# Strassen for a third unit, and the spectral steps moved one unit earlier

## The chip, the cores and the metric

One core of a Trainium2 chip runs the kernel. The metric is the device time of one execution in microseconds (us), lower is better. TensorE is called PE in the profile, its weight loads PEld, VectorE DVE, ScalarE ACT, GpSimd POOL and SyncE SP.

## The reference

The input `x` is (8, 3008, 256): batch, tokens, channels. All is float32.

```python
X = np.fft.rfft(x, axis=1)                         # over the 3008 tokens
Yr = Xr @ w_r - Xi @ w_i + b_r                     # mix of the 256 channels
Yi = Xr @ w_i + Xi @ w_r + b_i
Yr, Yi = soft_threshold(Yr, 0.01), soft_threshold(Yi, 0.01)
y = np.fft.irfft(Yr + 1j * Yi, n=3008, axis=1)     # (8, 3008, 256)
h = np.maximum(y.transpose(0, 2, 1) @ w_tok1, 0) @ w_tok2   # 3008 -> 256 -> 3008 tokens
u = y + h.transpose(0, 2, 1)
out = u + np.maximum(u @ w_ch1, 0) @ w_ch2         # 256 -> 1536 -> 256 channels
```

## The kernel before, in words

The eight batches form five units: unit 0 is batch 0, unit 1 is batch 1, units 2, 3 and 4 are pairs of batches. To hold float32 accuracy on the fast matmul format, an operand is split into a high and a low part, and a product is three matmuls (`mm3`, lines 191 to 194, so the profile names most matmuls by these lines and by their tiles).

Each unit passes two phases.

The *spectral phase* (`spectral`, with the closures of `parts`). First comes the transform `dft47`, a Fourier transform of length 47 in 13 groups. A group loads `x` (480 KB for a pair of batches, SP's queue, three buffers of tag `ld`), forms sums and differences (`sum_diff`, GpSimd and VectorE), splits them (`split_x`, ScalarE and VectorE), runs six matmuls (`stage1`, tile `p`), copies them out with ScalarE (tile `a`, line 265, two buffers of tag `ev`) and stores `a` to DRAM (`a_d`, line 267, ScalarE's queue). Unit 1 is half as wide. Then come 12 pairs of frequencies `kp`, for each batch: `forward` (tile `px`, line 465, then `xf`, `xth`, `xtl` by ScalarE, GpSimd, ScalarE and VectorE), `mix` (tiles `pm`), and once for each `kp` `inverse` (tiles `pi`, stored to `b_d`) and `tokens` (tile `gp`). `mix` of a step follows the `forward` of the next one. `close` turns `gp` into the hidden tokens `gh` and `gl`.

The *channel phase* (`channel`). `make_u` builds `u` from `gh`, `gl`, the second token weights `wt2` and `b2`, loaded from `b_d` (tile `pu`). A chunk of up to 512 tokens then takes, for each of 12 blocks of 128 hidden channels, six matmuls for the first layer (tile `ph`), a rectification and split (`hh` line 810, `hlo` line 811) and six matmuls for the second (tile `po`). The units of `SEVEN`, the last ones, use `channel7` instead: chunks of 1024 tokens, and the first layer as Strassen's scheme in Winograd's form, with seven products in place of eight (tiles `sx`, `sw`, `sq`, `sz`). It needs sums of the weights (`weigh`) and of `u` (`sum_u`, `split_u7`) and sums of the products (`first7`), done on VectorE and ScalarE. These units' tiles live in the pool `seven`, which `open_seven` opens where the spectral tiles were, so all spectral work must be over by then.

The order in each engine's queue is written out by the program. Unit 0's spectral phase stands alone at the start (`begin`), beside weight preparation. After that the spectral steps of later units are dealt out between pieces of the channel phase. `BESIDE` says whose steps run beside which unit. A loop at the end keeps `left_s` (spectral work left, by the plan 70.3 us a batch) and `left_c` (channel work left until the unit's last chunk), and after each channel piece emits steps:

```python
            while left_s > pace * left_c:
                step = next(sp, None)
                if step is None:
                    left_s = -1e9
                elif step == "wait":
                    hold = left_c - 10.0
                    break
                else:
                    left_s -= step
```

`pace` is `left_s / left_c`, taken anew after each hold. A step tells its planned time: 1.4 for a group of a pair unit's transform (0.7 for unit 1), 0.9 for `forward`, 2.15 for `mix`, 0.68 a batch for `inverse`, 1.37 a batch for `tokens`. A "wait" holds the spectral steps until 10 us of planned channel work have been emitted; before the change there is one, after each transform, for the way of `a` through DRAM. A chunk of 512 counts 32.7, a `make_u` 3.6 for 470 tokens. At "end", what is left of the steps is emitted at once. The first hold, in unit 0, is 25.

The hidden tokens of one unit at a time lie in the two tiles `gh` and `gl` of the pool `const`; those of units 3 and 4 are stored to DRAM (`g_d`) when made, and loaded by `fetch_g` when their channel phase comes.

Of the kernel before, what the change touches and what calls it, by code (L numbers as in the profile page):

```python
# [11 lines left out]
F32 = mybir.dt.float32  # L12
# [5 lines left out]
B, N, C = 8, 3008, 256  # L18
# [5 lines left out]
UNITS = [[0], [1]] + [[2 * p, 2 * p + 1] for p in range(1, NP)]  # L24
# [9 lines left out]
CH = N  # L34
NCH = 1
NF = DF // 128
SEVEN = (3, 4)
CW7 = 2 * CW
BESIDE = {0: [1], 1: [2], 2: [3, 4]}

# [83 lines left out]
def tile_kernel(ctx: ExitStack, tc: tile.TileContext, io):  # L126
    nc = tc.nc
    V, S, G, PE, DMA, PUT = nc.vector, nc.scalar, nc.gpsimd, nc.tensor, nc.sync, nc.scalar

    const = ctx.enter_context(tc.tile_pool(name="const", bufs=1))  # L130
    spectrum = ExitStack()
    mid = spectrum.enter_context(tc.tile_pool(name="mid", bufs=1, side="right"))
    wk = spectrum.enter_context(tc.tile_pool(name="wk", bufs=2, side="right"))
# [45 lines left out]
    def load_wide(src, n, pool=None, tag="o", raw=None, after=None):  # L179
        if raw is None:  # L180
            raw = load_raw(src, n, pool)
        rows = raw.shape[0]
        tmp = wk.tile([rows, 2, n], F32, tag=tag, name="wide", bufs={"o": 3, "hl": 4}[tag])
        if after is None:
            return narrow(raw, tmp[:, 0], tmp[:, 1])
        none = pool.tile([rows, 1], F32, name="none")
        V.tensor_scalar(out=none.bitcast(U32), in0=after[:rows, :1].bitcast(U32), scalar1=0, scalar2=None, op0=ALU.bitwise_and)
        V.tensor_copy(out=tmp[:1, :, 0], in_=after[:1])
        return narrow(raw, tmp[:, 0], tmp[:, 1], none)
# [9 lines left out]
    f1r = mid.tile([120, 2, 2, 128], F32R, name="f1r")  # L199
    f2 = mid.tile([128, 4, 96], F32, name="f2")  # L200
    g2 = const.tile([96, 2, 96], F32, name="g2")[:, :, :TOKS]
    sc = const.tile([128, 16], F32, name="sc")
    sc, lam = sc[:, :4], sc[:, 4:5]
    bias = mid.tile([128, 2, C], F32, name="bias")
    wmh = mid.tile([128, 3, 2, C], F32R, name="wmh")
    wml = mid.tile([128, 3, 2, C], F32R, name="wml")
# [20 lines left out]
    w_d = dram.tile([KP, 128, 2, DT], F32, name="w_d")  # L227
    a_d = [dram.tile([128, KH, 512], F32, name=f"a_d{p}") for p in range(2)]
    b_d = [dram.tile([NSLOT, 96, 512], F32, name=f"b_d{u}") for u in range(len(UNITS))]
    g_d = {u: dram.tile([2, 128, 2 * 2 * C], F32, name=f"g_d{u}") for u in SEVEN}  # L230

# [47 lines left out]

    def dft47(load, dst, w, ahead, eng, pool=None, turned=False):
        xs = [load(g) for g in range(ahead)]
        yield 0.0
        sds = {}

        def prepare(g):
            if g < NG:
                sds[g] = sum_diff(xs[g], g, w, eng, pool)
                xs[g] = None  # L290

        def divide(g):
            if g < NG and pool is None:
                sds[g] = split_x(sds[g], w)

        prepare(0)
        prepare(1)
        divide(0)
        for g in range(NG):
            if g + ahead < NG:  # L300
                xs.append(load(g + ahead))
            prepare(g + 2)
            divide(g + 1)
            if turned:
                stage1_turned(sds.pop(g), dst, g)
            else:
                stage1(sds.pop(g), dst, g, w, pool)
            yield 0.7 * w / C
# [102 lines left out]
    def fetch_g(u):  # L411
        gts[u] = [const.tile([128, 2, len(UNITS[u]), C], F32R, name=n, tag=n) for n in ("gh", "gl")]
        for i, g in enumerate(gts[u]):
            DMA.dma_start(out=g.rearrange("p j b c -> p (j b c)").bitcast(F32), in_=g_d[u][i])


    def parts(u):
# [3 lines left out]
        w = nb * C  # L421
# [111 lines left out]
                        mm3(gp[:, jt, :w], wt[:, 0, i, js], wt[:, 1, i, js], rows(y, 0, i), rows(y, 1, i), start, stop)  # L533

        def close():
            if u in SEVEN:
                gh, gl = hl([128, 2, nb, C], "gh"), hl([128, 2, nb, C], "gl")
            else:
                gh = const.tile([128, 2, nb, C], F32R, name="gh", tag="gh")
                gl = const.tile([128, 2, nb, C], F32R, name="gl", tag="gl")  # L540
            for j in range(2):
                hv, gv = gh[:, j].rearrange("p b c -> p (b c)"), acc[0][:, j, :w]
                S.activation(out=hv, in_=gv, func=AF.Relu)
                V.scalar_tensor_tensor(out=gl[:, j].rearrange("p b c -> p (b c)"), in0=gv, scalar=0.0, in1=hv.bitcast(F32), op0=ALU.max, op1=ALU.subtract)
            gts[u] = gh, gl
            if u in SEVEN:
                for i, g in enumerate(gts[u]):
                    PUT.dma_start(out=g_d[u][i], in_=g.rearrange("p j b c -> p (j b c)").bitcast(F32))

        return SimpleNamespace(**{k: v for k, v in locals().items()})  # L550

# [244 lines left out]
    def channel(n):  # L796
        u, at, cw = chunks[n]
        uf, uh, ul = us.pop(n)
        after = chunks[n + 1] if n + 1 < len(chunks) else None
        po = ps1.tile([128, 2, 512], F32, name="po")  # L800
        hs = {}

        def first(f):
            pt = bank("ph")[:, :cw]
            fs = slice(f * 128, (f + 1) * 128)
            for ct in range(2):
                mm3(pt, wc["w1"][:, 0][:, ct, fs], wc["w1"][:, 1][:, ct, fs], uh[:, ct, :cw], ul[:, ct, :cw], ct == 0, ct == 1)
            hh = wc["wk2"].tile([128, CW], F32R, name="hh", bufs=3)[:, :cw]
            hlo = wc["wk2"].tile([128, CW], F32R, name="hlo", bufs=3)[:, :cw]
            S.activation(out=hh, in_=pt, func=AF.Relu)  # L810
            V.scalar_tensor_tensor(out=hlo, in0=pt, scalar=0.0, in1=hh.bitcast(F32), op0=ALU.max, op1=ALU.subtract)  # L811
            hs[f] = hh, hlo

        def second(f):
            hh, hlo = hs.pop(f)
            for ct in range(2):
                cs = slice(ct * 128, (ct + 1) * 128)
                mm3(po[:, ct, :cw], wc["w2h"][:, f, cs], wc["w2l"][:, f, cs], hh, hlo, f == 0, f == NF - 1)

        for f in range(NF + 2):  # L820
            if f < NF:
                first(f)
            if f >= 2:
                second(f - 2)
            if n == 0:
                if f in late:
                    split_w2(*late.pop(f))
                if f % 2 == 0 and f // 2 + 2 < NF // 2:
                    late[f + 1] = f // 2 + 2, narrow_w2(f // 2 + 2)
            if after:  # L830
                mine = needs[n + 1]
                seven = after[0] in SEVEN
                if f == 0:
                    if seven:
                        yield "end"
                        open_seven()
                        fetch_g(after[0])
                    if mine:
                        load_wt2(mine[0])
                if f == 2:  # L840
                    if after[0] != u and not seven:
                        yield "end"
                    if mine:
                        load_b2(mine[0])
                if seven and f == 10:
                    load_ahead(n + 2)
                if seven and f in (1, 3, 5):
                    weigh(f // 2)
                first_at = 9 if len(mine) == 1 else 4 if seven else 6
                for i, g in enumerate(mine):  # L850
                    if f == first_at + 4 * i - (4 if i == 0 else 2):
                        split_wt2(g)
                    if f == first_at + 4 * i:
                        yield 3.6 * make_u(g) / GW
                        if i + 1 < len(mine):
                            load_wt2(mine[i + 1])
                            load_b2(mine[i + 1])
                if f == 10:
                    (sum_u if seven else split_u)(n + 1)
                if seven and f >= 10:  # L860
                    for i in range(2 * f - 20, min(7, 2 * f - 18)):
                        split_u7(n + 1, i)
            yield (1.37 if f in (0, 1, NF, NF + 1) else 2.73) * cw / CW
        if "seven" in wc:
            o = wc["seven"].tile([128, 2, CW], F32, tag="t7", name="o", bufs=1)
        else:
            o = wk.tile([128, 2, CW], F32, tag="o", name="o", bufs=3)
        step = 2 if after else 1
        for c in range(0, 2, step):
            cs = slice(c, c + step)  # L870
            V.tensor_tensor(out=o[:, cs, :cw], in0=po[:, cs, :cw], in1=uf[:, cs, :cw], op=ALU.add)
            for b, bi in enumerate(UNITS[u]):
                lo, hi = max(at, b * N), min(at + cw, (b + 1) * N)
                if lo < hi:
                    DMA.dma_start(out=outv[bi][:, cs, lo - b * N:hi - b * N], in_=o[:, cs, lo - at:hi - at])
# [163 lines left out]
    for n, (u, at, cw) in enumerate(chunks):  # L1039
# [3 lines left out]
        if at == 0:  # L1043
            if u:
                sp, done = chain.from_iterable(spectral(v) for v in BESIDE[u]), 0.0
            left_s = sum(len(UNITS[v]) for v in BESIDE[u]) * 70.3 - done
            mine = [w for cu, _, w in chunks if cu == u]
            made = sum(k for gu, _, _, k in groups if gu == u) - sizes[0]
# [57 lines left out]
```

## Time and profile before

| what | value |
|---|---|
| median of 3 runs | 2421.27 us (2420.08 to 2422.24) |
| profiled execution | 2420.28 us, span of its trace 2418.5 us |
| busy TensorE matmuls | 2392.1 us, 99% of the span |
| busy VectorE, ScalarE, GpSimd | 55%, 45%, 13% |
| moved by DMA | 250.29 MB, 103 GB/s on the mean |
| issues of `a_d<-a`, `x<-in_x` for pair units | 36 and 39, 480 KB each, median 5.1 and 4.8 us to landing |

Busy times count an engine's own instructions; waiting, branching and issuing of DMAs are not counted. Matmuls overlap in the pipeline, so the mean duration of one (384 ns on line 192) is longer than the time between two. A row of stretches gives, for each engine, the busy time and the count of instructions in it, then the granted TensorE clock as a share of full speed, the mean busy share of the 16 DMA engines and the rate. In a row of instructions the brackets tell how long the engine was idle before it and which event ended that.

### The profile page before, as it was taken

The numbers are of one execution on the slowest core, as the hardware profiler recorded it, in microseconds if no ns is written. First come the engines' busy times: TensorE is split into PE (matmuls) and PEld (weight loads), VectorE is DVE, ScalarE is ACT, GpSimd is POOL, SyncE is SP. The second block draws the span as 40 slices with busy tenths as digits, with TensorE's granted clock in tenths as the row PEclk, the third lists the DMA queues.
The fourth block names the chain that finished last, engine by engine and source line by source line (L and its number), as shares of the span: only waits on it lengthen the run. The fifth ranks groups of instructions, "written<-read, shape, count | busy, mean of one in ns | idle before, by whom it ended". The sixth has DMA issues, their size and how long they took to land.

```text
span 2418.5 us, 32134 instructions
## 1 busy us (share of the span) xinstructions
PE 2392.1 (99%) x12632; PEld 2079.9 (86%) x12632; DVE 1321.4 (55%) x2070; ACT 1082.1 (45%) x1931; POOL 308.4 (13%) x259
## 2 busy tenths in 40 slices
PE   8999999999999999999999999999999999999999
PEld 7878999988888888888788888898888889888887
DVE  7985655444544454444544444555555555555554
ACT  6764444443334343333443333354444444444543
POOL 0000222212222122222322222000000000000000
PEclk9999999999999999999999999999999999999999
DMA  8864345552233452323662321322311112221100
GB/s 210 252 216 146 96 123 143 154 166 91 85 94 99 134 168 91 106 89 91 186 186 81 95 87 47 119 72 59 90 57 37 54 54 81 60 87 59 38 2 34
DMA packets 145155, 250.29 MB, mean 103 GB/s; under 512 B 10421, under 2 KB 98317, under 8 KB 145005
## 3 DMA queue, kind: packets, MB, share of 16 engines
q1 hardware_dynamic: 114649, 192.67, 27.0%
q10 hardware_dynamic: 30356, 55.58, 7.1%
q8 instruction: 99, 1.62, 0.3%
q14 instruction: 51, 0.42, 0.1%
HBM read 161.84 MB, written 86.38 MB: 103 GB/s over the span
## 4 chain that ended last, share of the span: by engine, by line
PE 93%; DVE 3%; DMA 2%; ACT 1%; SPq 1%; issue 0%; POOL 0%; ACTq 0%; DVEq 0%; POOLq 0%
PE po L192 10%; PE po L194 10%; PE po L193 10%; PE ph L192 5%; PE ph L193 5%; PE ph L194 5%; PE pu L772 5%; PE px L465 3%; PE pm L192 2%; PE pm L194 2%; PE pm L193 2%; PE sx L192 2%; PE sx L194 2%; PE sx L193 2%; PE pu L192 2%; PE pu L194 2%
## 5 line engine op out<-in xcount | busy, mean ns | idle before, releaser
L192 PE MATMUL po<-hh,w2h 128*128 128x512 f32 (+4 forms) x1176 | 452.0, 384 | 0.0
L193 PE MATMUL po<-hlo,w2h 128*128 128x512 f32 (+4 forms) x1176 | 449.3, 382 | 0.0
L194 PE MATMUL po<-hh,w2l 128*128 128x512 f32 (+4 forms) x1176 | 449.3, 382 | 0.0
L811 DVE SCALAR_TENSOR_TENSOR hlo<-ph,hh 128x512 fp32r<-128x512 f32 (+4 forms) x300 | 196.7, 656 | 249.6 <-ACT hh L810 247.8
L810 ACT ACTIVATE hh<-ph 128x512 fp32r<-128x512 f32 (+4 forms) x300 | 171.4, 572 | 285.4 <-PE ph L194 280.7
L194 PEld LDWEIGHTS po<-hh,w2l 128*128 128x128 f32 x1176 | 220.9, 188 | 39.0
L192 PEld LDWEIGHTS po<-hh,w2h 128*128 128x128 f32 x1176 | 221.1, 188 | 38.3
L193 PEld LDWEIGHTS po<-hlo,w2h 128*128 128x128 f32 x1176 | 221.0, 188 | 37.8
L192 PE MATMUL ph<-uh,w 128*128 128x512 f32 (+4 forms) x600 | 230.9, 385 | 0.9 <-DVE hlo L811 0.9
L193 PE MATMUL ph<-ul,w 128*128 128x512 f32 (+4 forms) x600 | 228.1, 380 | 0.0
L194 PE MATMUL ph<-uh,w 128*128 128x512 f32 (+4 forms) x600 | 227.5, 379 | 0.0
L938 ACT ACTIVATE hh<-sn 128x512 fp32r<-128x512 f32 (+1 forms) x288 | 180.7, 627 | 58.0 <-DVE sn L958 37.9
L939 DVE SCALAR_TENSOR_TENSOR hlo<-sn,hh 128x512 fp32r<-128x512 f32 (+1 forms) x288 | 193.8, 673 | 7.0 <-ACT hh L938 0.6
L146 DVE TENSOR_TENSOR xtl<-xf,xth 128x768 fp32r<-128x768 f32 x84 | 81.4, 969 | 144.6 <-ACT xth L143 144.6
L947 DVE TENSOR_TENSOR sn<-sq,sn 128x512 f32<-128x512 f32 (+1 forms) x72 | 48.9, 680 | 199.3 <-PE sq L194 184.6
L192 PE MATMUL pm<-wmh,xth 128*128 128x256 f32 x504 | 146.2, 291 | 2.2 <-ACT xth L143 2.1
L943 ACT COPY sn<-sx 128x512 f32<-128x512 f32 (+1 forms) x72 | 41.6, 578 | 230.0 <-PE sx L194 229.9
L193 PE MATMUL pm<-wml,xth 128*128 128x256 f32 x504 | 142.1, 282 | 0.0
L194 PE MATMUL pm<-wmh,xtl 128*128 128x256 f32 x504 | 141.9, 283 | 0.0
L779 ACT COPY uf<-pu 128x470 f32<-128x470 f32 (+20 forms) x164 | 61.2, 406 | 175.3 <-PE pu L772 174.9
L146 POOL TENSOR_TENSOR yl<-z,yh 128x512 fp32r<-128x512 f32 x72 | 92.9, 1290 | 346.9 <-ACT yh L143 346.9
L772 PEld LDWEIGHTS pu<-g,b 96*128 96x128 f32 x1024 | 130.9, 191 | 3.3
(185 smaller groups left out, 4885.8 us busy)
## 6 DMA issues: line engine op xcount, KB each, us to landing
wt<-wt_d SPq DMA_DIRECT2D x28, 940.0 KB, 5.8
x<-in_x SPq DMA_DIRECT2D x39, 480.0 KB, 4.8
a<-a_d SPq DMA_DIRECT2D x36, 512.0 KB, 3.8
b_d<-bt ACTq DMA_DIRECT2D x36, 512.0 KB, 3.3
a_d<-a ACTq DMA_DIRECT2D x36, 480.0 KB, 5.1
wt<-wt_d SPq DMA_DIRECT2D x21, 752.0 KB, 5.3
b<-b_d SPq DMA_DIRECT2D x32, 480.0 KB, 6.4
aw<-w_d SPq DMA_DIRECT2D x48, 256.0 KB, 2.7
```

The source lines that it names most:

```text
L146: lo_eng.tensor_tensor(out=lo, in0=src, in1=hi.bitcast(F32), op=ALU.subtract)
L192: PE.matmul(out, lhsT=wh, rhs=xh, start=start, stop=False, skip_group_check=more)
L193: PE.matmul(out, lhsT=wh, rhs=xl, start=False, stop=False, skip_group_check=more)
L194: PE.matmul(out, lhsT=wl, rhs=xh, start=False, stop=stop, skip_group_check=more)
L465: PE.matmul(pt[:, o:o + 128], lhsT=x, rhs=f2cols(2 * kp + ab), start=True, stop=True)
L772: PE.matmul(pt[:, s * TOKS:(s + 1) * TOKS], lhsT=b2[:, s, cs], rhs=g2[:, 0 if s0 + s == 0 else 1], start=False, stop=s == k - 1)
L779: S.copy(out=ufs[m][:, ct, lo - at:hi - at], in_=pt[:, lo - c0:hi - c0])
L810: S.activation(out=hh, in_=pt, func=AF.Relu)
L811: V.scalar_tensor_tensor(out=hlo, in0=pt, scalar=0.0, in1=hh.bitcast(F32), op0=ALU.max, op1=ALU.subtract)
L938: S.activation(out=hh, in_=t, func=AF.Relu)
L939: V.scalar_tensor_tensor(out=hlo, in0=t, scalar=0.0, in1=hh.bitcast(F32), op0=ALU.max, op1=ALU.subtract)
L947: V.tensor_tensor(out=snap[0], in0=q, in1=snap[0], op=ALU.add)
```

## The change

Unit 2 joins the Strassen units: `SEVEN` becomes (2, 3, 4). As the spectral phases must be over before these begin, they move up: those of units 1 and 2 run beside unit 0, those of units 3 and 4 beside unit 1, and none beside unit 2. (The list of the units that run in the plain form is now 0 and 1.) The hidden tokens of units 1 to 4 go through DRAM (`SPILL`). Each transform whose sums use GpSimd (units 2, 3, 4) begins with a "wait" after its first three loads. A tile `edge` of 32 bytes is put at the right end of the memory, which shifts the tiles of the right-hand pools by as much, and the column `none` moves from a tile of its own into free columns of the tile `sc`.

```diff
-SEVEN = (3, 4)
+SEVEN = (2, 3, 4)
+SPILL = (1, 2, 3, 4)
 CW7 = 2 * CW
-BESIDE = {0: [1], 1: [2], 2: [3, 4]}
+BESIDE = {0: [1, 2], 1: [3, 4]}
...
+    edge = ctx.enter_context(tc.tile_pool(name="edge", bufs=1, side="right"))
+    edge.tile([128, 8], F32, name="edge")
...
-        none = pool.tile([rows, 1], F32, name="none")
+        wc["none"] = wc.get("none", 4) + 1
+        none = wide_sc[:rows, wc["none"]:wc["none"] + 1]
...
-    sc = const.tile([128, 16], F32, name="sc")
-    sc, lam = sc[:, :4], sc[:, 4:5]
+    wide_sc = const.tile([128, 16], F32, name="sc")
+    sc, lam = wide_sc[:, :4], wide_sc[:, 4:5]
...
-    g_d = {u: dram.tile([2, 128, 2 * 2 * C], F32, name=f"g_d{u}") for u in SEVEN}
+    g_d = {u: dram.tile([2, 128, 2 * 2 * C], F32, name=f"g_d{u}") for u in SPILL}
...
     def dft47(load, dst, w, ahead, eng, pool=None, turned=False):
         xs = [load(g) for g in range(ahead)]
-        yield 0.0
+        yield "wait" if eng is G else 0.0
...
         def close():
-            if u in SEVEN:
+            if u in SPILL:
                 gh, gl = hl([128, 2, nb, C], "gh"), hl([128, 2, nb, C], "gl")
...
-            if u in SEVEN:
+            if u in SPILL:
                 for i, g in enumerate(gts[u]):
-                    PUT.dma_start(out=g_d[u][i], in_=g.rearrange("p j b c -> p (j b c)").bitcast(F32))
+                    PUT.dma_start(out=g_d[u][i, :, :2 * w], in_=g.rearrange("p j b c -> p (j b c)").bitcast(F32))
...
                 if f == 2:
                     if after[0] != u and not seven:
                         yield "end"
+                        if after[0] in SPILL:
+                            fetch_g(after[0])
...
             if u:
                 sp, done = chain.from_iterable(spectral(v) for v in BESIDE[u]), 0.0
+            else:
+                sp = chain(sp, *(spectral(v) for v in BESIDE[u][1:]))
```

More of the change, by code (lines that the diff above doesn't have):

```diff
@@ L413, in fetch_g @@
         for i, g in enumerate(gts[u]):
-            DMA.dma_start(out=g.rearrange("p j b c -> p (j b c)").bitcast(F32), in_=g_d[u][i])
+            DMA.dma_start(out=g.rearrange("p j b c -> p (j b c)").bitcast(F32), in_=g_d[u][i, :, :2 * len(UNITS[u]) * C])
     def parts(u):
```

## The prediction

> **What bounds the kernel now.** I read the page first (busy shares, the chain that ended last), then busy time by stage, then by stretch around the places where TensorE was not full, then the waits and the chain inside those stretches.
>
> ```profile
> span 2418.5 us, 32134 instructions
> PE 2392.1 (99%) x12632; PEld 2079.9 (86%) x12632; DVE 1321.4 (55%) x2070; ACT 1082.1 (45%) x1931; POOL 308.4 (13%) x259
> PE 93%; DVE 3%; DMA 2%; ACT 1%; SPq 1%; issue 0%; POOL 0%; ACTq 0%; DVEq 0%; POOLq 0%
> ```
>
> TensorE is the bound: 93% of the chain and nearly always busy. So a change pays by taking matmul columns away, and costs by making TensorE wait. The stages by stretch (us; busy time and count of PE, PEld, DVE, ACT, POOL; granted clock; DMA share; GB/s): unit 0, unit 1, unit 2, the two Strassen units, and 50 us inside the last.
>
> ```profile
> 154.10:456.00 301.90, 299.64 (x1811) 281.75 (x1811) 178.62 (x315) 130.09 (x243) 50.98 (x40) 1.00 0.43 128
> 456.00:827.70 371.70, 368.35 (x1995) 320.91 (x1994) 177.97 (x250) 149.33 (x257) 88.32 (x73) 1.00 0.38 115
> 827.70:1569.60 741.90, 738.19 (x4021) 643.34 (x4021) 371.19 (x519) 302.55 (x522) 166.33 (x140) 1.00 0.37 115
> 1569.60:2418.50 848.90, 844.54 (x4025) 716.46 (x4023) 468.05 (x723) 396.34 (x723) 0.00 (x0) 1.00 0.19 56
> 2350.00:2400.00 50.00, 50.00 (x219) 40.90 (x218) 27.57 (x41) 22.51 (x40) 0.00 (x0) 1.00 0.06 22
> ```
>
> The little idle time there is lies mostly in the transforms (`dft47`). The next rows are those of unit 1 (its last ten groups), 2, 3 and 4, then two stretches inside.
>
> ```profile
> 184.70:208.50 23.80, 23.26 (x133) 20.60 (x132) 20.27 (x41) 15.04 (x29) 0.00 (x0) 1.00 0.63 181
> 458.40:505.40 47.00, 44.22 (x206) 37.95 (x206) 26.45 (x29) 28.68 (x45) 15.65 (x9) 0.96 0.73 217
> 829.90:875.10 45.20, 44.61 (x235) 40.66 (x234) 30.35 (x34) 30.31 (x50) 15.18 (x9) 1.00 0.77 232
> 1184.90:1234.00 49.10, 47.05 (x206) 37.73 (x205) 33.57 (x35) 30.49 (x47) 19.61 (x11) 0.97 0.77 240
> 1206.00:1213.00 7.00, 7.00 (x32) 5.69 (x31) 5.22 (x6) 4.97 (x8) 3.54 (x3) 1.00 0.98 314
> 493.00:500.00 7.00, 4.22 (x13) 2.98 (x12) 3.11 (x4) 3.54 (x6) 1.77 (x1) 0.82 0.63 202
> ```
>
> What TensorE waited for at 496 us: the chain inside that stretch, and below it the waits of 465 to 505 us (total, times, longest):
>
> ```profile
> 488.71 7.66 DMA a_d<-a
> 496.45 0.60 ACT a L265
> 497.09 0.50 PE p L192
> ```
> ```profile
> ACT a L265 <- DMA a_d<-a: 9.2, 3, 4.8
> PE p L192 <- ACT a L265: 2.5, 1, 2.5
> ```
>
> The transform's result tile `a` has two buffers; ScalarE's copy into one waits until the store of two groups earlier has landed, and TensorE, in order, waits behind it.
>
> **Strassen for unit 2: a gain.** 219 matmuls filled 50.00 us, 228 ns each, nearly all of 512 columns. Unit 2's first layer was 6016 tokens x 12 blocks x 6 matmuls = 433,152 columns, 846 times 512. With seven products it is, per token half, 6 pairs x 7 x 3 = 126 matmuls over 3008 columns = 379,008, or 740.25 times 512. 105.75 fewer x 0.228 = **-24.1 us**. The second layer and the making of `u` keep their columns. The extra vector work is hidden already in the Strassen stage: PE 844.5 of 848.9 us, DVE 468.05 (55%).
>
> **The spectral steps, packed denser: the cost.** Their matmuls stay the same. What changes is the channel work between them, set by the pacing loop as left_s / left_c. Unit 0 has left_c = 32.7 x 2632/512 + 3.6 x 27 x 94/470 + 0.5 = 188, unit 1 has 179. Following the holds (25, then 10 at each wait), spectral work per channel work is: unit 1 transform 1.28 (68.2/163 = 0.42 before), unit 2 transform 1.51 and steps 1.73 (0.78 and 0.84 before), unit 3 1.66 and 1.77 (0.71 and 0.75), unit 4 2.03 and 2.43 (under 0.8).
>
> A transform of a pair unit has 13 groups x 6 matmuls x 0.228 = 17.8 us, and it counts 18.2 in the plan, so the channel work between its groups is 18.2/1.51, 18.2/1.66, 18.2/2.03 = 12.0, 11.0, 9.0. TensorE's own time for them becomes 29.8, 28.8 and 26.8 us; the stretches took 47.0, 45.2 and 49.1. Can the transfers follow? Here are ScalarE's copies in order of time:
>
> ```profile
> 470.17 1.08 ACT L265 COPY a<-p 120x512 f32<-120x512 f32 x2 [2.15 <-DMA a_d<-a]
> 472.92 1.08 ACT L265 COPY a<-p 120x512 f32<-120x512 f32 x2 [0.17 <-PE p L194]
> 478.16 1.07 ACT L265 COPY a<-p 120x512 f32<-120x512 f32 x2 [2.22 <-DMA a_d<-a]
> ```
>
> And the issues with their landings (median us, last figure): at 1199 to 1222 us, then the stores alone after 1219 us, then unit 1's at 186 to 208.
>
> ```profile
> a_d<-a ACTq DMA_DIRECT2D x7, 480.0 KB, 5.3
> x<-in_x SPq DMA_DIRECT2D x6, 480.0 KB, 6.3
> ```
> ```profile
> a_d<-a ACTq DMA_DIRECT2D x3, 480.0 KB, 3.4
> ```
> ```profile
> a_d<-a ACTq DMA_DIRECT2D x9, 240.0 KB, 3.4
> ```
>
> One buffer is taken for 1.1 us of copies and 5.3 us until the store lands; two buffers give a group each (1.1 + 5.3)/2 = 3.2 us while inputs flow, and (1.1 + 3.4)/2 = 2.3 for the last three, when they don't. The copies at 470 and 478 us show 4.0 a group. The DMA engines agree: 960 KB a group at 314 GB/s and 0.98 busy is 3.1 us. So 10 x 3.2 + 3 x 2.3 = 38.9 us a transform, whatever TensorE would like: stalls of 9.1 + 10.1 + 12.1 = 31.3 us. Unit 1's ten groups: half as wide, 10 x 6 x 0.114 + 7/1.28 = 12.3 us of TensorE against 2.0 ((0.6 + 3.4)/2) to 2.4 (23.8/10) a group; at 2.2, 22 us: 9.7 more. Off go the idle times of the four rows before, 0.5 + 2.8 + 0.6 + 2.0 = 6.0. Sum **+35.0**. The new wait ahead of each transform is no instruction: it holds the plan for 10 us of channel work, under which the first three inputs land; the other ten still have to come.
>
> The low end is the byte rate, 10 x 3.1 + 3 x 1.55 (stores only) = 35.7 a transform, and nothing for unit 1: 107.1 - 85.4 - 6.0 = +16. The high end is 4.0 a group (46.9) and 2.4 for unit 1: 140.7 - 85.4 + 11.7 - 6.0 = +61. I take 3.2, the value of most landings.
>
> A rule of the Trainium skill sits beside the byte rate. "DMA: Bandwidth & Descriptors", section Specifications, gives HBM about 358 GB/s a core; by it a group is 960/358 = 2.7 us, an estimate, and the sum would be near 2424. The busiest row stood at 314 with the engines at 0.98, so I stay with the rows.
>
> **Half clock.** The granted clock was 0.82 over 493 to 500 us, after the wait of 2.5. Over the transforms, 0.96 x 47.0 and 0.97 x 49.1 lost 1.9 + 1.5 = 3.4 us. I add 2: more such windows, partly inside time that waits anyway. Ends 0 and +10.
>
> **The steps themselves.** From `forward` to `mix` data pass four engines:
>
> ```profile
> 1428.92 1.06 PE L465 MATMUL px<-f,a 128*128 128x128 f32 x8
> 1430.02 0.59 ACT L467 COPY xf<-px 128x512 f32<-128x512 f32 x1 [1.67 <-PE px L465]
> 1430.75 0.74 POOL L468 TENSOR_TENSOR xf<-xf 128x256 f32<-128x256 f32 x1 [5.11 <-ACT xf L467]
> 1431.52 0.84 ACT L143 CAST xth<-xf 128x768 fp32r<-128x768 f32 x1 [0.92 <-POOL xf L468]
> 1432.39 0.96 DVE L146 TENSOR_TENSOR xtl<-xf,xth 128x768 fp32r<-128x768 f32 x1 [0.96 <-ACT xth L143]
> ```
>
> From the end of the px matmuls (1429.98) `xth` takes 2.4 us and `xtl` 3.4. On TensorE one mix and the next forward lie between, 2.15 + 0.9 by the plan, and in every second step nothing else is sure to. `xtl` is read by the third matmul, so about 0.3 us can be missing there: 36 such steps, half of them without a channel piece between. With some queueing I take **+5**; low 0, high +23 (one channel operation ahead on ScalarE and VectorE, 1.3 us, in 18 steps).
>
> **At nothing.** SP's queue: a chunk's output store stands in it until VectorE has made `o`, and loads issued later stand behind.
>
> ```profile
> SPq L875 <- DVE o L871: 9.1, 1, 9.1
> ```
>
> TensorE meets that `o` at the same place of its own order, and a step's loads are issued a pair of frequencies (10.2 us of spectral work by the plan, more with channel work) ahead of their use, against a landing of 3.8 us (row of `a` below); uncovered it would be that, once a chunk, 11 times. The spills: stores and loads of 512 KB take 3.1 to 4.4 us and `make_u` comes four block steps (11 us) after the fetch; uncovered they would be 9 us in two units. The constant `none`: at worst its write waits for the `sc` load beside `fw`.
>
> ```profile
> fw<-in_fw SPq DMA_DIRECT2D x1, 128.0 KB, 10.4
> raw<-in_moe_w_ch SPq DMA_DIRECT2D x12, 512.0 KB, 4.2
> a<-a_d SPq DMA_DIRECT2D x36, 512.0 KB, 3.8
> g_d<-gh ACTq DMA_DIRECT2D x2, 512.0 KB, 3.1
> gl<-g_d SPq DMA_DIRECT2D x2, 512.0 KB, 4.4
> ```
>
> They write other columns, so I take 0, high +10. The `edge` tile moves all right-hand tiles by 32 bytes, onto whole 64-byte lines. `raw` mostly sat on such lines before, `a` did not, and `a` (3.8) lands no later than `raw` (4.2), so 0; at best 0.4 us off each of 30 groups, -12. Opening the Strassen pool moves one unit earlier; its place, the last chunk with no spectral work, is the same.
>
> **Sum.** -24.1 + 35.0 + 2 + 5 = +17.9. On the profiled execution's 2420.28 us (span 2418.5) that is 2438; its time is 1.0 under the median of the runs shown, so **2439 us**.
>
> **The rivals.**
> *The transforms keep their cover* (other side: faster). Stores and inputs run at the low end, prefetch fills more, steps lose nothing: -24 + 16 = 2412; with cover as today, 2396. It decides once the transforms and the steps together stall less than 24 us more than today. For it: at 830 us only 0.6 us was idle at DMA 0.77. Against: the 0.98 row. Chance 0.25, with all sums under -5.
> *Nothing to see*: stalls take what Strassen gives, 2416 to 2425. Chance 0.10.
> *The steps or the clock go too*: steps at +23 and transforms at the high end, -24 + 61 + 23 + 8 = 2488; from 2466 up. Chance 0.09. The Trainium skill's "TensorE: Matmul & The Clock Gate", section on HAM oscillation, warns of idle gaps over about 3.4 us; this trace shows half clock after 2.5.
> *VectorE becomes the bound*: against it, unit 1 held 178 us of DVE in 372; a second pair's work, (371.2 - 178.0) less channel work, adds at most 193 in 144 of TensorE: 72% of 516. Chance 0.01.
>
> **Numbers.** Forecast 0.55 (2425 to 2466). Faster by over 0.2% (about what a measurement of this kernel can tell from no change, 4.8 us) 0.25, within 0.10, slower 0.65. The range 2404 to 2470 leaves out the far ends of the first and third rival.
>
> **What would show it.** The Strassen units' stretch near 1273 us (1.5 x 848.9). The three transforms at 36 to 42 us each with PE busy near 75%, DMA share over 0.85, and `ACT a` waiting for `a_d<-a` as the top wait. Granted clock there under 0.95. `pm` waiting for `xth` or `xtl` under 10 us in all. The prediction is wrong if the transforms last under 33 us, or if the steps between `forward` and `mix` wait longer than the transforms do.

## The result, and the profile after

The changed kernel takes **2437.21 us** (median; the kernel before, on the same chips, 2420.68): a ratio of 1.0067, 95% interval 1.0051 to 1.0084. Slower by 0.7%, and 1.8 us under the forecast of 2439. The profiled execution took 2437.33 us, its span 2435.5. That the total fits is partly luck: of the prediction's terms one (Strassen) is right, one (the transforms) is somewhat too large and rests on a mechanism that is only a third of it, one (the steps) is far too small, and one that was put at nothing (the edge tile) gave most of that back.

From the page after: span, TensorE's busy time, and the chain that ended last.

```profile
span 2435.5 us, 32450 instructions
PE 2379.9 (98%) x12524; PEld 2063.7 (85%) x12524; DVE 1442.1 (59%) x2256; ACT 1176.7 (48%) x2105; POOL 309.1 (13%) x259
PE 84%; DMA 6%; DVE 4%; ACT 3%; issue 2%; POOL 1%; SPq 1%; ACTq 0%; DVEq 0%; POOLq 0%
```

TensorE is busy 12 us less, the span is 17 us longer, and the chain runs through TensorE for 84%, not 93%. The stages after (unit 0, unit 1, the three Strassen units; columns as before), then the four transforms (the last ten groups of unit 1's; those of units 2, 3 and 4):

```profile
154.20:629.30 475.10, 454.02 (x2728) 414.29 (x2728) 302.35 (x475) 226.14 (x404) 138.78 (x113) 0.99 0.49 149
629.30:1170.80 541.50, 525.15 (x2946) 454.15 (x2945) 310.42 (x429) 250.66 (x424) 167.57 (x140) 0.99 0.43 133
1170.80:2435.50 1264.70, 1260.29 (x6069) 1078.43 (x6067) 703.99 (x1089) 597.15 (x1091) 0.00 (x0) 1.00 0.19 58
```
```profile
184.80:206.00 21.20, 17.16 (x90) 14.56 (x89) 14.35 (x30) 11.35 (x21) 0.00 (x0) 0.88 0.72 208
348.50:388.80 40.30, 35.19 (x144) 25.61 (x143) 31.53 (x41) 28.11 (x45) 15.91 (x9) 1.00 0.82 251
648.90:694.40 45.50, 39.48 (x173) 30.54 (x172) 28.05 (x26) 28.09 (x46) 16.15 (x9) 0.96 0.79 239
909.20:947.70 38.50, 32.90 (x116) 22.01 (x115) 24.10 (x23) 24.02 (x38) 16.11 (x9) 0.91 0.74 220
```

The reader is to see two things. Units 0 and 1, beside which all the spectral steps now run, take 1016.6 us together where units 0 to 2 took 1415.5, but the idle time in these stages has grown from 9.3 us to 37.4 (lengths less PE busy). And the transforms, thinned out, run with TensorE idle 4 to 6 us each and at granted clocks down to 0.88.

To compare kernels I use one measure, called *excess*: the time by which the matmuls start later than at the undisturbed start-to-start spacing of their shape (227 ns for 512 columns), summed over a stretch. It counts idle time and half-clock time alike. Worked out from each trace:

| kernel (profiled) | excess in transforms | excess elsewhere, while spectral work runs | Strassen stage |
|---|---|---|---|
| before | 14.3 | 16.9 | 848.9 (two units) |
| after | 40.6 | 36.4 | 1264.7 (three) |
| rise | +26.3 | +19.5 | |

The matmuls themselves, at undisturbed spacing, fell by 23.4 us (from 2217.5 over these stages to 2194.1). The Strassen stage's own excess fell from 11.0 to 5.4, though it has a unit more. So -23.4 + 26.3 + 19.5 - 5.6 = +16.8, against 17.0 between the spans.

### The profile page after: what moved, and what is told of

Its sections match the earlier page's. It is cut to its first block, busy times and chain, and to the rows that moved or that the text cites. A ratio compares the mean times of both kernels' runs of the same rounds, so it can differ in the third digit from the quotient of the medians.

```text
span 2435.5 us, 32450 instructions
## 1 busy us (share of the span) xinstructions
PE 2379.9 (98%) x12524; PEld 2063.7 (85%) x12524; DVE 1442.1 (59%) x2256; ACT 1176.7 (48%) x2105; POOL 309.1 (13%) x259
## 4 chain that ended last, share of the span: by engine, by line
PE 84%; DMA 6%; DVE 4%; ACT 3%; issue 2%; POOL 1%; SPq 1%; ACTq 0%; DVEq 0%; POOLq 0%
PE po L196 10%; PE po L198 10%; PE po L197 10%; PE pu L776 5%; DMA a_d<-a 3%; PE sx L196 3%; PE sx L198 3%; PE sx L197 3%; PE ph L196 2%; PE ph L197 2%; PE ph L198 2%; PE px L469 2%; PE sw L196 2%; PE sw L198 2%; PE sw L197 2%; PE pu L196 2%
## 5 line engine op out<-in xcount | busy, mean ns | idle before, releaser
L196 PE MATMUL po<-hh,w2h 128*128 128x512 f32 (+3 forms) x1176 | 453.0, 385 | 0.0
L197 PE MATMUL po<-hlo,w2h 128*128 128x512 f32 (+3 forms) x1176 | 449.5, 382 | 1.4 <-DVE hlo L815 1.4
L198 PE MATMUL po<-hh,w2l 128*128 128x512 f32 (+3 forms) x1176 | 448.7, 382 | 0.0
L944 ACT ACTIVATE hh<-sn 128x512 fp32r<-128x512 f32 (+1 forms) x432 | 270.8, 627 | 86.3 <-DVE sn L964 56.7
L945 DVE SCALAR_TENSOR_TENSOR hlo<-sn,hh 128x512 fp32r<-128x512 f32 (+1 forms) x432 | 290.3, 672 | 10.1 <-ACT hh L944 0.6
L815 DVE SCALAR_TENSOR_TENSOR hlo<-ph,hh 128x512 fp32r<-128x512 f32 (+3 forms) x156 | 98.9, 636 | 98.5 <-ACT hh L814 98.2
L814 ACT ACTIVATE hh<-ph 128x512 fp32r<-128x512 f32 (+3 forms) x156 | 86.7, 556 | 105.3 <-PE ph L198 101.2
L776 PE MATMUL pu<-g,b 96*128 96x94 f32 x1024 | 129.2, 271 | 0.0
L196 PE MATMUL ph<-uh,w 128*128 128x512 f32 (+3 forms) x312 | 120.5, 387 | 1.9 <-DVE z L498 1.0
L146 ACT CAST xth<-xf 128x768 fp32r<-128x768 f32 x84 | 70.1, 835 | 102.0 <-POOL xf L472 101.9
```

Source lines behind the costliest of these rows:

```text
L146: S.copy(out=hi, in_=src)
L196: PE.matmul(out, lhsT=wh, rhs=xh, start=start, stop=False, skip_group_check=more)
L197: PE.matmul(out, lhsT=wh, rhs=xl, start=False, stop=False, skip_group_check=more)
L198: PE.matmul(out, lhsT=wl, rhs=xh, start=False, stop=stop, skip_group_check=more)
L776: PE.matmul(pt[:, s * TOKS:(s + 1) * TOKS], lhsT=b2[:, s, cs], rhs=g2[:, 0 if s0 + s == 0 else 1], start=False, stop=s == k - 1)
L944: S.activation(out=hh, in_=t, func=AF.Relu)
```

## The experiments

Times are medians, with the ratio to the kernel before and its 95% interval. The kernel before took 2420.6 us beside e1 to e4, 2419.7 beside e5 to e8, 2421.1 beside e9 to e11 and 2419.5 beside e12.

**1 and 2. The edge tile, taken out and put in alone.**

```
e1_after_noedge: after, without
-    edge = ctx.enter_context(tc.tile_pool(name="edge", bufs=1, side="right"))
-    edge.tile([128, 8], F32, name="edge")
e2_before_edge: before, with these two lines (and the constant none placed in sc)
```

> The changed kernel without the 32-byte tile at the edge; everything else as changed. Theory: the shift by 32 bytes made the matmuls of the Strassen products faster (about 233 ns from start to start before, 227 after), so it hides a gain inside the result. Then this kernel is slower than the changed one by 2268 products x 5 ns = 11 us, near 2448, and its products take 231 to 235 ns again. Rival: the products run faster for another reason (no spectral work left beside them, other neighbours in memory); then it stays within 3 us of 2437 and the products keep 227 ns.

> The kernel before with the edge tile alone (and the constant none moved into the tile sc to make room); nothing of the schedule moves. Theory: 1512 products at 5 ns less, 8 us, and perhaps 1 or 2 us in the spectral matmuls: near 2411. Rival: no effect, 2420.

Without it the kernel after takes 2449.91 us (1.0121, 1.0103 to 1.0138): 12.7 more. With it the kernel before takes 2412.18 (0.9959, 0.9944 to 0.9974): 8.4 less, already faster than both. Both are near what was expected, and come to 4.2 us for each Strassen unit. Fifty microseconds inside the last unit, the same place of the code: after, after without the tile, before with it (before had 219 matmuls, shown above).

```profile
2367.00:2417.00 50.00, 50.00 (x222) 41.41 (x221) 27.85 (x42) 22.87 (x40) 0.00 (x0) 1.00 0.06 22
```
```profile
2378.00:2428.00 50.00, 50.00 (x219) 40.91 (x218) 27.58 (x41) 22.52 (x40) 0.00 (x0) 1.00 0.06 22
```
```profile
2343.70:2393.70 50.00, 50.00 (x223) 41.39 (x222) 27.95 (x42) 22.80 (x40) 0.00 (x0) 1.00 0.06 22
```

DMA is at 0.06 in all three, so this isn't a matter of transfers. A Strassen product of 512 columns starts every 232.2 ns without the tile and every 227.6 with it, in both kernels. It is these products alone, whose operand `ub` lies in a right-hand pool: those of the second layer (`po`), whose operands lie on the left, start every 227 ns (median) in all four kernels, and so do those of `gp<-yh,wt`, although their tiles moved by the same 32 bytes.

**3. The move alone.** Strassen for two units as before, the spectral steps where the change puts them.

```
-SEVEN = (2, 3, 4)
+SEVEN = (3, 4)
-BESIDE = {0: [1, 2], 1: [3, 4]}
+BESIDE = {0: [1, 2], 1: [3, 4], 2: []}
```

> The changed kernel, but unit 2 in the plain form with no spectral work beside it: the spectral steps are moved, Strassen's scheme is not extended. Theory: the matmuls saved are worth 24 us and the faster products of the third unit another 0 to 4, so this is 2437 + 24 to 28 = 2461 to 2465. Rival: the third Strassen unit costs something of its own (sums on VectorE, the pool opened earlier), and this kernel is nearer, 2450.

2463.09 us (1.018, 1.0158 to 1.0201). With experiment 2 this takes the change apart, edge tile in all: edge -8.4 (2420.6 to 2412.2), move **+50.9** (to 2463.1), Strassen for the third unit **-25.9** (to 2437.2). The sum is +16.6. By their intervals the last two are good to some 6 us each; the four runs of this kernel lie between 2459.6 and 2471.8.

**4. Four store buffers for the pair units' transforms.**

```
+        if pool is None and w == 512 and g % 2:
+            a = wk.tile([120, 2, w], F32, tag="wt", name="a", bufs=2)
```

> The changed kernel with four buffers instead of two for the transform's result tile a in the pair units (every other group takes a buffer of the idle tag wt). Theory of the prediction: two buffers held until the store lands set 3.2 us a group; with four the transforms of units 2 to 4 come down to what the DMA rate allows (960 KB at 314 GB/s, 3.1 us) or less: 38 to 45 us now, 32 to 38 then, 10 to 15 us off in all, near 2425. Rival A, the byte rate alone: nothing changes, within 3 us of 2437, and the waits go from the store to the input loads. Rival B, the chain of splits on ScalarE and VectorE (TensorE waits most for xl): within 3 us too, with no wait on any DMA left.

2427.78 us (1.0028, 1.0018 to 1.0039): 9.4 less, just short of the 10 to 15 expected. ScalarE's waits for a store, 15.3 and 22.8 us in units 0 and 1 after the change, go in the three pair units' transforms (the 8.3 us left lie in unit 1's, which keeps two buffers), and the excess of the three transforms falls from 32.5 to 21.4. So the store buffers were a third of it, and the DMA engines had room: with four buffers the three transforms moved 264, 269 and 239 GB/s, with two 251, 239 and 220. The two waits after the change, and the transforms of this kernel:

```profile
ACT a L269 <- DMA a_d<-a: 15.3, 11, 2.7
```
```profile
ACT a L269 <- DMA a_d<-a: 22.8, 9, 3.8
```
```profile
351.50:389.50 38.00, 33.31 (x142) 25.69 (x142) 34.54 (x41) 28.14 (x44) 15.91 (x9) 1.00 0.82 264
651.10:690.70 39.60, 36.35 (x170) 29.27 (x169) 28.98 (x26) 28.34 (x46) 16.19 (x9) 1.00 0.84 269
906.00:941.10 35.10, 31.68 (x118) 23.12 (x117) 28.07 (x23) 25.39 (x39) 16.16 (x9) 0.90 0.74 239
```

**5 to 7. Where do the 19.5 us outside the transforms come from?** In unit 0 ScalarE waits for the raw second token weights (7.8 us in 4 waits at `wide`, where there were 1.8 before). My theory was that SP's queue makes them late.

```profile
ACT wide L160 <- DMA raw<-in_wt: 7.8, 4, 2.5
```

```
e5_no_narrow: unit 0's second token weights, channel phase
-            wfs[g] = [load_wide(io["wt2"][0, jt][:, cols], k * TOKS, pool) for jt in range(2)]
+            (raw words into a tile of tag "o"; the high words are taken as they are)
e6_g_loads: in the spectral steps
-                    ws[kp + 2] = load_w(w_d, kp + 2), load_e(kp + 2)
+                    ws[kp + 2] = load_w(w_d, kp + 2, G), load_e(kp + 2, G)
e7_after_a4_g: e4 and e6 together, the extra buffers in unit 1's transform too (tag "et")
```

> The kernel after, without the narrowing of unit 0's second token weights: their raw words are loaded into three buffers of the tag o, and the high words are used as they lie, so the ACT and VectorE work of load_wide falls away there (the output is not the reference's). Theory A (late weights): the excess outside the transforms of unit 0, 24.5 us after the change against 6.0 before, is these raw loads arriving late and holding up ACT and VectorE, which wait for them in order. The excess falls to 8 to 12 us and the time from 2437 to 2421 to 2427. Theory B (density): unit 0 simply carries more steps than ACT and VectorE can do beside a shorter product stream; narrowing is a small part of their work, the excess stays above 20 us and the time at 2433 to 2438.

> The kernel after, with the step's loads of w and e two iterations ahead issued from GpSimd's queue and not from SyncE's; nothing else is changed. Theory A1 (SyncE's queue): the second token weights are late because the loads in front of them on SyncE's queue wait for a buffer (24.5 us and 47.8 us of queue wait in the window from 205 to 350 us). With those elsewhere the weights are early again: unit 0's excess outside the transforms falls from 24.5 to 8 to 16 us, the time to 2423 to 2430. Theory A2: the weights are late for another reason (their own buffer comes free late, or the transfers are slow): the time stays within 4 us of 2437. A loss is possible, because GpSimd's own work waits behind its queue: above 2441 would say that this costs more than SyncE's queue does.

> Both repairs together on the kernel after: every second group of every transform beside the work takes its store buffer from another tag (four in all, unit 1's transform too), and the step's loads of w and e are issued from GpSimd's queue. If the two causes are separate, the gains add: 9.4 us for the buffers (2427.8 with them alone), 1 to 3 us for unit 1's transform, and what the loads alone bring (7 to 14 us by theory A1): 2412 to 2420, no slower than the kernel before. If SyncE's queue is no cause (A2), 2425 to 2430.

Without the narrowing, which leaves the low words of unit 0's weights out: 2429.96 us (1.0044, 1.0031 to 1.0057), 7 less; the excess of unit 0 outside transforms goes from 24.5 to 16.7 (in a profiled execution 6 us under that median). That is between the two theories: the narrowing matters, but is not most of it. The loads on GpSimd's queue: 2450.32 (1.013, 1.0108 to 1.0151), 13 *more*, and both repairs 2433.85 (1.0056, 1.0039 to 1.0073), 6 more than the buffers alone and above all that was expected. With the loads moved, ScalarE's 7.8 us of waits at `wide` are gone, so SP's queue had a part in the lateness. But unit 0's excess outside the transforms, which theory A1 had falling to 8 to 16 us, does not fall: it is some 3 us higher than after the change. What the lateness alone costs TensorE is not shown, because the move has a cost of its own. The waits of 154 to 1171 us in the kernel with the loads alone moved (e6) say which: GpSimd now stands waiting for load buffers, and ScalarE waits longer (127.7 against 101.9 us after the change) for GpSimd's `xf`.

```profile
POOL ef L358 <- DVE et L149: 85.7, 31, 8.4
ACT xth L146 <- POOL xf L472: 127.7, 81, 5.9
```

This pointed at GpSimd's place in the forward chain. In order of time, the kernel after, unit 0 (start, duration, engine, line, [idle before and what ended it]):

```profile
285.48 1.29 POOL L149 TENSOR_TENSOR y<-z,y 128x512 fp32r<-128x512 f32 x1 [7.40 <-ACT y L146]
285.54 1.49 DVE L168 TENSOR_SCALAR wide<-wide 128x470 uint32<-128x470 uint32 x1
285.83 0.56 ACT L814 ACTIVATE hh<-ph 128x470 fp32r<-128x470 f32 x1
286.72 1.46 POOL L149 TENSOR_TENSOR wt<-aw,wt 128x512 fp32r<-128x512 f32 x1
286.95 1.50 DVE L166 TENSOR_SCALAR wide<-raw 128x470 uint32<-128x470 uint32 x1
288.14 0.90 POOL L472 TENSOR_TENSOR xf<-xf 128x256 f32<-128x256 f32 x1
...
289.07 0.83 ACT L146 CAST xth<-xf 128x768 fp32r<-128x768 f32 x1 [2.21 <-POOL xf L472]
...
290.58 0.39 DVE L168 TENSOR_SCALAR wide<-wide 128x470 uint32<-128x470 uint32 x1
...
290.90 0.63 DVE L815 SCALAR_TENSOR_TENSOR hlo<-ph,hh 128x470 fp32r<-128x470 f32 x1
...
291.58 0.39 PE L196 MATMUL pi<-y,et 128*128 128x256 f32 x1 [1.84 <-DVE hlo L815]
```
```profile
289.00:293.00 4.00, 2.15 (x15) 1.74 (x14) 4.00 (x9) 1.42 (x2) 0.04 (x1) 1.00 0.67 197
293.00:296.40 3.40, 3.40 (x14) 3.07 (x13) 3.40 (x6) 2.44 (x5) 0.40 (x1) 0.50 0.85 229
296.40:300.00 3.60, 3.60 (x27) 3.40 (x26) 2.42 (x6) 1.67 (x3) 3.60 (x2) 1.00 0.25 71
```

`hh` is done at 286.4, but `hlo` starts at 290.90: it stands behind the narrowing on VectorE, two of whose operations (lines 168 and 166) take 1.49 and 1.50 us while GpSimd works; line 168 takes 0.39 when it doesn't. `xf` stands behind two other operations on GpSimd, so ScalarE is held 2.21 us at `xth`. TensorE waits 1.84 us, and 1.4 us after that runs at half clock for 3.4 us, 14 matmuls where the next 3.6 us hold 27. None of this appears as a wait of TensorE for `xth` or `xtl`.

**9 and 10. GpSimd taken out, at two places** (each on top of the four store buffers).

```
e9_after_a4_sd: sum_diff, each group's sum
-        eng.tensor_tensor(out=sd[:, 0], in0=x[:, 0], in1=x[:, 1], op=ALU.add)
+        V.tensor_tensor(out=sd[:, 0], in0=x[:, 0], in1=x[:, 1], op=ALU.add)
e10_after_a4_xf: forward, the third row
-            (V if plain else G).tensor_tensor(out=xf[:, 0], in0=xf[:, 1], in1=xf[:, 2], op=ALU.add)
+            V.tensor_tensor(out=xf[:, 0], in0=xf[:, 1], in1=xf[:, 2], op=ALU.add)
```

> The kernel after with four store buffers (2427.8 us, transforms beside the work at 38.0, 39.6 and 35.0 us), and the sum of each group made by VectorE and not by GpSimd. Theory C (split chain): what is left of the stalls there is TensorE waiting for xl, which VectorE makes in 1.75 to 2.0 us while GpSimd's 1.8 us sum runs and in 1.22 us otherwise. VectorE would take on 0.69 us a group and save 0.5 to 0.8 on xl, and one hand-over between engines goes: the three transforms shorten by 2 to 5 us each, the time to 2415 to 2423. Theory D (bytes): the rest of the stall is the DMA engines at a share of 0.77 to 0.84, which this leaves alone: the transforms stay within 1 us, the time at 2426 to 2430. If VectorE, busy for 28 to 34 of 34 to 38 us there, is full, the transforms grow: above 2432.

> The kernel after with four store buffers, and the third spectral row (xf) of each forward step formed by VectorE and not by GpSimd. Theory E (the forward chain): of the excess outside the transforms in units 0 and 1, 15.5 us are waits of the mixing products for xth and xtl, which follow px over ACT, GpSimd's xf (0.75 us behind ACT's copy, ACT waits for it 16.4 us in the window 205 to 349 us alone) and ACT again. Without GpSimd's part the chain is 0.4 to 0.8 us shorter: the pm excess falls from 15.5 to under 9 us, the time from 2427.8 to 2419 to 2424. Rival F: VectorE's queue, in front of which z and xtl stand, takes over the wait: the pm excess stays within 2 us, the time at 2426 to 2430.

The sums on VectorE: 2418.53 us (0.9993, 0.9984 to 1.0002), 9 less. `xl` at its longest falls from 2317 to 1226 ns (rows of the tile, with four buffers and then with the sums moved), and the three transforms shorten by 2.4, 1.4 and 3.3 us (2 to 5 were expected) while their DMA share goes up. Theory C holds; D, that bytes set the rest, does not for this part.

```profile
L149 DVE TENSOR_TENSOR xl<-sd,xh x52: 680/1226/2317, 135.9 to 938.2; 120x1024 fp32r<-120x1024 f32 x39, 120x512 fp32r<-120x512 f32 x13
```
```profile
L149 DVE TENSOR_TENSOR xl<-sd,xh x52: 679/1218/1226, 134.3 to 922.2; 120x1024 fp32r<-120x1024 f32 x39, 120x512 fp32r<-120x512 f32 x13
346.20:381.80 35.60, 33.42 (x142) 25.70 (x141) 32.51 (x50) 27.68 (x44) 0.00 (x0) 1.00 0.85 282
640.00:678.20 38.20, 36.15 (x170) 29.24 (x169) 28.23 (x35) 27.90 (x47) 0.00 (x0) 1.00 0.86 279
893.50:925.30 31.80, 28.81 (x118) 21.20 (x117) 25.78 (x32) 24.90 (x39) 0.00 (x0) 1.00 0.79 264
```

`xf` on VectorE: **2407.9 us** (0.9941, 0.9928 to 0.9954), 20 less than with the buffers alone, more than the 4 to 9 that I expected. The excess outside the transforms falls from 36.6 to 17.1 us, to what it was before the change (16.9). If each delay is booked at the matmul that starts late, the mixing products (`pm`) fall from about 15 us to under 6, as theory E expected, and another 11 us go at `pi`, `ph` and `gp`, the products behind them. Rival F falls. The waits over 154 to 1171 us with four buffers, and with `xf` moved as well:

```profile
ACT xth L146 <- POOL xf L475: 102.0, 83, 2.3
DVE xtl L149 <- ACT xth L146: 99.7, 60, 5.6
```
```profile
ACT xth L146 <- DVE xf L475: 52.9, 62, 1.5
DVE xtl L149 <- ACT xth L146: 18.7, 49, 1.1
```

So the forward chain with GpSimd in it is the cause of the rise outside the transforms: it costs the delay of `pm` itself, and the hold on ScalarE and VectorE, with `hh`, `hlo`, `bt` behind it. One thing the experiment doesn't part: without GpSimd's `xf`, VectorE's own operations also run shorter (lines 508 and 509 on `z`: 107.3 us in all with four buffers, 97.7 with `xf` moved).

**8, 11 and 12. The repairs on the kernel before, and all together on the kernel after.** e8: the edge tile and four store buffers (in all transforms beside the work) on the kernel before. e11: e8 with the sums on VectorE. e12: the kernel after with the edits of e4, e9 and e10.

> The kernel before, with the 32-byte edge tile and with four store buffers in the transforms beside the work. The edge alone gave 2412.2 us. The transforms of the kernel before have an excess of 1.6, 5.7, 1.6 and 5.4 us over their matmuls at undisturbed spacing, 14.3 in all: if the wait for a store buffer makes as large a part of it as it did after the change (a third to a half), 4 to 7 us go: 2405 to 2408. If in these transforms the store is no cause (it lands ahead of need beside the slower stream), 2411 to 2413.

> The kernel before with the edge tile and four store buffers (2401.6 us), and the sum of each group made by VectorE. There the transforms have only 6 us of excess left, 0.6 to 2.7 each, so by theory C at most 3 us go: 2398 to 2402; by theory D nothing: 2401 to 2403.

> The kernel after with all three repairs: four store buffers, each group's sum and the forward step's third row xf on VectorE. If the two VectorE edits are independent, their gains over 2427.8 us add (9.3 and 19.9): 2396 to 2401, at or below the repaired kernel before (2401.6). If VectorE becomes full where both lie together, which they do not (the sums lie in the transforms, xf in the steps between them), or if the steps now reach the next limit, 2402 to 2408.

e8: **2401.61 us** (0.9922, 0.9905 to 0.9938), 10.6 less than with the edge alone and more than the 4 to 7 expected. The transforms' excess fell from 12.7 to 5.9 as expected, and no half-clock stretch is left beside the work; of the 12.6 us between the two profiled spans another 4.7 lie ahead of 158 us, where the edge-only kernel had a stretch of half clock. Its profiled execution is the slowest of its six (2407.0 to 2414.0), so part of this may be that run alone. e11: 2401.81 (0.9918, 0.9904 to 0.9931), nothing more, which both theories allowed. e12: 2401.89 (0.992, 0.9907 to 0.9933), 3 above the sum of its parts, which the intervals don't tell from nothing; its excess is 23.4 in the transforms and 17.7 elsewhere.

Two versions thus beat the kernel before by 0.8%, one with the change and one without it, and they are equal: repaired, the move still costs about what Strassen's third unit gives. Their repairs are not the same, though: e8 has four buffers in unit 1's transform too, and the kernel before with `xf` on VectorE was not run.

## Why the prediction was right, and where it was not

**Strassen, -24.1: right.** The third unit gave 25.9, good to some 6 us, between two kernels that differ in it alone. Of this 23.5 us are matmuls at undisturbed spacing (105.75 fewer products, as counted).

**Transforms, +35.0, and half clock, +2: 10 us too much, and a third of the mechanism.** The three pair units took 39.4, 44.6 and 38.5 us (first to last matmul) where 38.9 each was forecast, and their excess is 8.9 + 11.1 + 12.5 = 32.5 against 31.3. Unit 1's is 8.1 against 9.7. What was mis-sized is what goes off: 6.0 us, taken from the idle times of four stretches, where the measure that counts half clock too has 14.3. The rise was 26.3. The wait for the store buffer, to which I gave all of it, is a third: with four store buffers 21.4 of the 32.5 us stay, and taking GpSimd's sum away leaves 14.2. So it is partly luck that 32.5 came so near to 31.3. The byte rate doesn't explain the rest as I had it: its low end was 35.7 us a transform, and unit 4's then took 31.8. But the DMA share rose to 0.79 to 0.86, and what holds the remaining 14.2 was not settled.

**The steps, +5: the term that failed.** It was +19.5 (36.4 against 16.9), near my high end of +23. I sized it by what TensorE could miss of `xth` and `xtl`, 0.3 us in 36 steps, and wrote that these waits would stay under 10 us. In the waits of 154 to 1171 us after the change they did, beside other waits of TensorE there:

```profile
PE pm L196 <- ACT xth L146: 2.8, 6, 0.7
PE pm L198 <- DVE xtl L149: 2.7, 6, 0.5
PE pi L196 <- DVE hlo L815: 3.5, 2, 1.8
PE pi L196 <- ACT bt L523: 2.8, 1, 2.8
```

These rows show a small part of the cost, for two reasons. A row counts only the idle time after the end of the matmul before, and matmuls overlap: by their starts, the mixing products are late by about 15 us, where it was 5 before. And ScalarE and VectorE, which work in order, are held at `xth` and `xtl` and delay what stands behind: about 8 us of the rise is at `pi`, which waits for `hlo` and `bt` in these rows, and 3 at `ph`. In experiment 10 both parts shrink with GpSimd's `xf` gone. The prediction's high end, "one channel operation ahead on ScalarE and VectorE", came near to it, and I took a value near the low one.

**At nothing.** SP's queue: it made the second token weights late (7.8 us of ScalarE's time), but no run shows what that cost TensorE; relieving it through GpSimd gained nothing, and other edits to it were not tried. The edge tile: wrong, -8.4 on the kernel before and -12.7 on the kernel after. I had its possible gain at -12 but on the loads of `a`; it lies in the Strassen products. The spills, `none` and the earlier pool were not tried alone, and the Strassen stage shows no cost of theirs: it lasts 1264.7 us, 1.5 times the 841.4 it lasts with the edge tile on the kernel before, plus 2.6.

**The sum.** By medians the move came to +50.9 where 35 + 2 + 5 = 42 was forecast, Strassen to 1.8 more than forecast, the edge tile to -8.4 where nothing was: 8.9 too little and 10.2 too much cancel, which is luck. Without the edge tile the change is 2449.9 us, 11 above the forecast and still inside the range.

**What would show it.** Strassen stage near 1273: 1264.7, shorter by the edge tile. Transforms 36 to 42 us: one at 45. PE busy near 75%: 85 to 87%, since busy time holds the half-clocked matmuls. DMA share over 0.85: it was 0.74 to 0.82; the DMA engines had room. Granted clock under 0.95: 0.91 in one, 1.00 and 0.96 in the others. `ACT a` waiting for `a_d<-a` is ScalarE's longest wait in each transform (7.3, 11.2 and 11.6 us), but TensorE itself waits there mostly for the splits `xl` and `xh`. Neither sign of being wrong came: no transform is under 33 us, and the steps' excess (36.4 us) stays under the transforms' (40.6). The rivals: "transforms keep their cover" is what e12 comes near to, with the transforms and steps repaired.

## What to carry to other kernels

Price a chain of short operations over several engines also by what stands *behind* it in the in-order queues, and not by the wait rows of its own reader alone: here 5.5 us in those rows stood for a rise of 19.5, and one small operation moved off GpSimd gave 20. When a stage is packed denser, look for the engine that is nearly idle but slow and in the middle (GpSimd, 30% busy in units 0 and 1); its latency is what the cover had hidden. And try each small companion of a large change alone: the edge tile's two lines were worth 8 to 13 us.

## What the runs showed of the hardware

*A shift of 32 bytes was worth 2% on some products.* Moving the right-hand tiles by 32 bytes changed the spacing of the Strassen products of 512 columns from 232.2 to 227.6 ns in both kernels, at a granted clock of 1.00. By the addresses the right-hand tiles come to lie on whole 64-byte lines. That is not a rule for every product: `gp`, moved by as much, stayed at 227. Why the Strassen products alone gain was not settled, and other offsets were not tried.

*VectorE is held while GpSimd works.* 0.39 us became 1.49 beside GpSimd's `y` of 1.29, and `xl` went from 1.23 to as much as 2.3. The Trainium skill, "SBUF — State Buffer", section Who interferes with whom, says that VectorE, in a mode that uses two ports, and GpSimd share a port pair which the first to issue holds for its whole instruction, blocking the other, and that a VectorE instruction with two inputs in SBUF contends with a GpSimd instruction that reads SBUF. The traces agree: the two long operations shown at line 168 and line 166 end 0.26 and 0.27 us after GpSimd's `y` and `wt`, and `xl` has two inputs in SBUF.

*Half clock after less than 2 us of idle time.* 2.15 us busy in 4.0, the longest wait 1.84, brought 3.4 us at 0.50. The Trainium skill, "TensorE: Matmul & The Clock Gate", section HAM oscillation, gives idle gaps over about 3.4 us as what to avoid; here far shorter ones did it. Beside the work two such stretches were there before, five after, one in e12 and none in e8. In the 3.4 us ahead of each of the seven, TensorE had been idle for 1.7 to 2.5 us in all.
